# Attention and mixture of experts on one core: side work as emission threads, batch 1's loads moved, fill matmuls recounted

## The chip, the cores and the metric

The kernel runs on one core of one Trainium2 chip. The core has a matmul engine, TensorE (PE in the rows; PEld is its loading of stationary operands, which overlaps the matmuls), and three engines for element-wise work: VectorE (DVE), ScalarE (ACT) and GpSimd (POOL). SyncE (SP) issues the DMA transfers; its queue is SPq in the rows. Every engine executes its own list of instructions in order and waits on semaphores for the others. The metric is the device time of one execution in microseconds (us), lower is better.

## What is computed

Eight batches of 576 tokens go through an attention in two steps and then, token by token, through one of eight experts. Cut to what matters:

```python
def sm_attn(qq, kk, vv):
    s = scale * np.matmul(qq, kk.transpose(0, 1, 3, 2))
    a = np.exp(s - np.max(s, axis=-1, keepdims=True))
    a = a / (np.sum(a, axis=-1, keepdims=True) + 1e-09)
    return np.matmul(a, vv)
p_packed = sm_attn(p, k, v)              # p: 8 x 8 x 32 x 64;  q, k, v: 8 x 8 x 576 x 64
x = sm_attn(q, p_packed, p_packed)       # then 8 x 576 x 512
logits = np.einsum('bsd,de->bse', x, w_gate)                    # 8 experts
local_gate = 1.0 / (1.0 + np.exp(-np.einsum('bsd,de->bse', x, w_local).squeeze(-1)))
for b in range(B):
    prev_e = -1
    for s in range(S):
        fresh_e = int(np.argmax(logits[b, s]))
        e = fresh_e if s == 0 or local_gate[b, s] < 0.5 else prev_e
        prev_e = e
        h = np.maximum(x[b, s] @ w1[e], 0.0)                    # 512 -> 1024
        out[b, s] = softmax(logits[b, s])[e] * (h @ w2[e])      # 1024 -> 512
```

## The kernel before

**Work of one batch.** The 32 packed queries p attend to the keys (`scores`, the products at L374), the weights are raised to the exponent and transposed (`keys`, L419) and multiplied with the values (L428); a last transpose (L443) leaves `ppT`, the packed values turned, one tile for each of two groups of heads. The real queries are multiplied with `ppT` (`queries`, L469), and VectorE, ScalarE and GpSimd make the attention weights a2 of them: `a2t` in full, `a2h` its rounded high part (ScalarE, L509) and `a2l` the remainder (L512; on GpSimd, but for the second group of batch 0, which is on VectorE). GpSimd then copies 64 columns (L513), so that a2t is a whole number of 128-column blocks long, 640. The attention output itself is never formed: the gate weights are folded into `ppT` (`gate_weights`, L529, tile `gs`), and the gate products (`gates`, L600) are `a2t` times `gs`. The first token's expert is taken for the whole batch; a path behind a condition redoes tokens that need another one, and it isn't taken with these inputs. VectorE writes the expert's number (L543), SyncE reads it into a register (L546) and issues the two halves of w1 (`weights`, L689) and the eight blocks of w2 (L695). In the same way w1 is folded: `pack_weights` (L712) multiplies `ppT` with each half of w1, and ScalarE and VectorE split the result into a high part `wph` (L719) and a remainder `wpl` (L722).

**The main stream.** `chunks` goes over the 1,024 hidden units in eight chunks of 128. For each it makes two halves of 288 tokens of the hidden layer (`layer1`, L736, six matmuls a half: high by high, remainder by high, high by remainder, for two groups); ScalarE takes the relu (L741) and VectorE the remainder (L747, in `rest`). The matrix w2 is split likewise (`split`, L835 and L837). Then the products with w2 of the chunk before are added into five accumulators, acc0 to acc4 (`layer2`, L762, and L767 and L771 for the last 64 tokens). After chunk 7 `store` scales each accumulator by the gate's probability `pe` and writes it out.

**What sets the order.** Each engine's list is written when the program is built. `weave` holds a set of generators, each with a condition under which it may go on (`need`): `chunks` is the main one; others, for up to three batches at once, are loads, weights, packing, keys, scores, gates and queries. `Clock` estimates when each tile will be ready, from prices of instructions and rates of transfers, and `weave` lets the main one and the others take turns by these estimates and by a credit. Inside `chunks` the relu's remainder, the two parts of the split and the stores are written at fixed places between the blocks of `layer2` (`also`). SyncE's transfers stand in one list too: for batch 1 the first values come first, and `loads` holds back keys, packed queries and queries until all of batch 0's w2 is issued.

**The opening.** Before batch 0's first chunk there is nothing dense to multiply. `keep_warm` (L206) writes matmuls of zeros into a spare accumulator: five at the start, more when the estimated share of matmul time falls below a half, and, before each estimated wait, as many as the wait has stretches of 800 ns. Batch 0 differs in other ways (`early`): its keys are loaded in token order, its expert is found ahead of the queries by `early_choice` (L555 and L577) from the first token alone, and its queries are turned (L454) after that.

## Time and profile before

| | |
|---|---|
| median of 3 runs | 445.09 us (445.06 to 445.36) |
| the profiled execution | 444.92 us, of which the span of the profile is 443.1 |
| mean granted TensorE clock over the span | 0.970 |
| TensorE busy | 420.3 us, 95% |
| VectorE busy | 310.4 us, 70% |
| ScalarE busy | 177.0 us, 40% |
| GpSimd busy | 32.3 us, 7% |
| moved by DMA | 73.13 MB, 165 GB/s on average |

The profile is one execution. Its rows give instructions with start and length, or groups of them with the sum of busy time, the mean, and what ended the idle time ahead of them. The granted clock is TensorE's share of full speed (0.50 is 1.2 GHz, 1.00 is 2.4 GHz). A table by stage gives these for stretches of the span: batch 0's chunks run from 44.1 us to 84.3, batch 1's from 103.1 on, and from 202.5 to 427.7 the steady batches follow each other without a break.

### The profile page before, as it was taken

Reading aid. Unit: us, or ns where it says so; the run is one execution under the profiler, and the core shown is the slowest. Engines: PE = TensorE matmul, PEld = TensorE weight load, DVE = VectorE, ACT = ScalarE, POOL = GpSimd, SP = SyncE. Lnnn points to the kernel's source line nnn. Section 1 sums busy time; section 2 is a strip of 40 time slices with the busy share of each in tenths; the row PEclk is TensorE's granted clock in tenths of the full one; section 3 lists DMA queues with packets and bytes.
Section 4 is the critical chain, followed back from the end, with each engine's and each line's share of the span. In section 5 each row is a group of like instructions: output and inputs, shape, how many; then the busy total and the mean of one; then the engine's idle time right before and its main releaser. Section 6 shows DMA issues by size and latency. Waiting matters only on the chain.

```text
span 443.1 us, 9660 instructions
## 1 busy us (share of the span) xinstructions
PE 420.3 (95%) x3694; PEld 318.4 (72%) x3695; DVE 310.4 (70%) x834; ACT 177.0 (40%) x395; POOL 32.3 (7%) x55
## 2 busy tenths in 40 slices
...
GB/s 193 149 300 257 128 178 122 65 197 300 114 189 331 185 123 205 117 321 121 158 107 316 194 128 185 127 325 114 162 96 323 153 15 0 187 240 62 1 1 112
DMA packets 179380, 73.13 MB, mean 165 GB/s; under 512 B 151424, under 2 KB 158336, under 8 KB 179328
## 3 DMA queue, kind: packets, MB, share of 16 engines
...
q8 instruction: 31, 0.51, 0.6%
q10 hardware_dynamic: 2128, 0.15, 0.4%
q14 instruction: 21, 0.17, 0.2%
...
## 4 chain that ended last, share of the span: by engine, by line
PE 86%; DVE 6%; DMA 3%; ACT 1%; SPq 1%; issue 1%; POOL 0%; POOLq 0%; DVEq 0%
PE acc L762 41%; PE bank L736 23%; PE bank L712 3%; PE acc L767 3%; PE acc L771 3%; PE bank L428 3%; PE bank L469 2%; PE bank L419 2%; PE bank L374 2%; DMA kv<-in_k_dram 2%; PE bank L600 1%; DMA qn<-in_q_dram 1%; SPq L274 1%; PE acc L206 1%; DVE a L381 1%
## 5 line engine op out<-in xcount | busy, mean ns | idle before, releaser
L762 PE MATMUL acc<-w2s,h 128*128 128x512 f32 x768 | 208.0, 402 | 0.0
L762 PEld LDWEIGHTS acc<-w2s,h 128*128 128x128 f32 x768 | 134.9, 188 | 38.1 <-issue 13.8
L741 ACT ACTIVATE h<-bank 128x288 fp32r<-128x288 f32 x128 | 52.6, 411 | 166.7 <-PE bank L736 161.5
L747 DVE SCALAR_TENSOR_TENSOR h<-bank,h 128x288 fp32r<-128x288 f32 (+2 forms) x192 | 61.5, 348 | 54.4 <-ACT h L741 54.0
L736 PE MATMUL bank<-a2h,wph 128*128 128x288 f32 x256 | 78.7, 307 | 1.0 <-ACT a2h L509 0.4
L736 PE MATMUL bank<-a2h,wpl 128*128 128x288 f32 x256 | 76.4, 298 | 0.8 <-DVE wpl L722 0.8
L736 PE MATMUL bank<-a2l,wph 128*128 128x288 f32 x256 | 75.7, 296 | 1.1 <-POOL a2l L512 1.1
L736 PEld LDWEIGHTS bank<-a2h,wph 128*128 128x128 f32 x256 | 48.5, 189 | 19.7 <-issue 6.0
L736 PEld LDWEIGHTS bank<-a2l,wph 128*128 128x128 f32 x256 | 48.7, 190 | 5.7 <-POOL a2l L512 1.3
L736 PEld LDWEIGHTS bank<-a2h,wpl 128*128 128x128 f32 x256 | 48.6, 190 | 1.2 <-DVE wpl L722 1.2
L837 DVE TENSOR_TENSOR w2s<-w2raw,w2s 128x512 fp32r<-128x512 f32 x64 | 43.2, 675 | 5.6 <-ACT w2s L835 5.2
L512 POOL TENSOR_TENSOR a2l<-a2t,a2h 128x576 fp32r<-128x576 f32 x15 | 21.4, 1426 | 313.5 <-ACT a2h L509 278.6
L835 ACT CAST w2s<-w2raw 128x512 fp32r<-128x512 f32 x64 | 39.2, 613 | 0.2
L767 PE MATMUL acc<-w2s,h 128*128 128x512 f32 x64 | 25.8, 403 | 0.0
L771 PE MATMUL acc<-w2s,h 128*64 128x512 f32 x64 | 25.3, 396 | 0.0
L719 ACT CAST wph<-bank 128x512 fp32r<-128x512 f32 x30 | 16.1, 589 | 18.1 <-PE bank L712 18.1
L454 DVE STREAM_TRANSPOSE qn<-qn 128x1152 f32<-128x1152 f32 x16 | 21.8, 1367 | 0.5 <-DMA qn<-in_q_dram 0.5
L476 DVE STREAM_TRANSPOSE sT<-bank 128x288 f32<-128x288 f32 x31 | 13.2, 462 | 12.1 <-PE bank L469 11.9
L722 DVE TENSOR_TENSOR wpl<-bank,wph 128x512 fp32r<-128x512 f32 x30 | 19.2, 682 | 2.3 <-ACT wph L719 2.3
L500 DVE TENSOR_TENSOR sT<-sT,sm 128x576 f32<-128x576 f32 x16 | 18.9, 1187 | 0.3
L342 DVE STREAM_TRANSPOSE qn<-qn 128x1152 f32<-128x1152 f32 x14 | 19.0, 1357 | 0.1
L406 ACT ACTIVATE a<-a,nb 128x576 f32<-128x576 f32 x16 | 12.3, 772 | 11.4 <-DVE nb L392 11.4
(135 smaller groups left out, 411.8 us busy)
## 6 DMA issues: line engine op xcount, KB each, us to landing
...
kv<-in_v_dram SPq DMA_DIRECT2D x16, 576.0 KB, 10.5
...
```

The lines of the kernel that those rows point to most:

```text
L342: nc.vector.transpose(out=kT, in_=kT)
L454: nc.vector.transpose(out=qT, in_=qT)
L512: eng.tensor_tensor(out=a2l, in0=a2t[:, 0:S], in1=a2h.bitcast(F32), op=ALU.subtract)
L722: nc.vector.tensor_tensor(out=lo[:, Q], in0=ts[Q], in1=hi[:, Q].bitcast(F32), op=ALU.subtract)
L736: nc.tensor.matmul(out=t[:, :HALF], lhsT=st["wp"][c // 4][wi][:, Q, fs], rhs=a2[ai][Q][:, ts], start=(n == 0), stop=(n == 5),)
L741: nc.scalar.activation(out=h[:, ts], in_=t[:, :HALF], func=AF.Relu)
L747: nc.vector.scalar_tensor_tensor(out=h[:, dst:dst + z - a], in0=t[:, a:z], scalar=0.0, in1=h[:, HALF * half + a:HALF * half + z].bitcast(F32),
L762: nc.tensor.matmul(out=acc, lhsT=hs[hi], rhs=w[:, wi], start=(c == 0 and n == 0), stop=(c == NC - 1 and n == 2),)
L767: nc.tensor.matmul(out=acc, lhsT=h[:, 512:S + TAIL], rhs=w[:, 0], start=(c == 0), stop=False, skip_group_check=True,)
L771: nc.tensor.matmul(out=acc[0:TAIL], lhsT=h[:, 512:S], rhs=w[:, 1], start=False, stop=(c == NC - 1), skip_group_check=True,)
L835: nc.scalar.copy(out=w[:, 0], in_=raw)
L837: nc.vector.tensor_tensor(out=w[:, 1], in0=raw, in1=w[:, 0].bitcast(F32), op=ALU.subtract)
```

## The change

It has five parts.

1. **Threads.** What `chunks` wrote at fixed places is now a generator of its own, handed over with `aside`: `relu` (with the remainder), `split` and `store`. `weave` places them by the estimates, as it does the others. The blocks of `layer2` wait for the halves that they read.
2. **Loads.** Packed queries come before the keys in every batch but 0. For batch 1 keys are issued once two of batch 0's w2 blocks are, and queries once four are (`FIRST_W2`); the later w2 blocks wait for that.
3. **Gates.** From batch 1 on the gate weights are nine more columns in the bank of the queries' products, copied out by ScalarE into one of three kept tiles (`gate_all`). a2t is 576 columns long and GpSimd's copy is gone: the gate products are eight of 128 columns and eight of 32. Batch 1's no longer wait for batch 0's `pe` in the planner, and batch 0's chain behind its gates stands behind batch 1's choice.
4. **Opening.** A wait is filled with one matmul for each 450 ns. Both remainders of a2 go to VectorE in batch 0, and one of two copies behind the transposes too; 1/s is formed after the transposes instead of before; both groups' exponents are written before the first transposes.
5. **Turns.** Generators that want a PSUM bank may run twice as far ahead of ScalarE's and VectorE's estimated work; transfers are placed first; until batch 1's expert is chosen the credit doesn't hold the others back.

```diff
+FIRST_W2 = {"k": 2, "q": 4}
+GW = E + 1
...
+    gate_all = [const.tile([128, NQ, 32], F32, name=f"gate{x}") for x in range(3)]
...
-            order = (("v", 0), ("v", 1), ("k", 1), ("q", 1))
+            order = (("v", 0), ("v", 1), ("p", 1), ("k", 1), ("q", 1))
         for name, Q in order:
             blocks = name == "q" or (name == "k" and not st["early"])
-            if isinstance(b, int) and b == 1 and name == "k":
-                yield need(when=lambda: "w2" in sts[0])
-            yield need(slot="qn" if blocks else "kv")
+            if isinstance(b, int) and b == 1 and name in FIRST_W2:
+                yield need(when=lambda: len(sts[0].get("w2", ())) >= FIRST_W2[name])
...
         for r in range(2):
-            yield need(sc, banks=1)
+            yield need(sc, banks=1, when=lambda: not st["early"] or st["weighed"] == NQ)
...
-            nc.scalar.copy(out=a1T[:, J3 * r:J3 * r + J3],
-                           in_=tp[:TP, :128 * J3].rearrange("a (j x) -> a j x", j=J3))
+            copy = nc.vector.tensor_copy if st["early"] and r == 1 else nc.scalar.copy
+            copy(out=a1T[:, J3 * r:J3 * r + J3], in_=tp[:TP, :128 * J3].rearrange("a (j x) -> a j x", j=J3))
...
+        if not st["early"]:
+
+            for h in range(HQ):
+                nc.tensor.matmul(
+                    out=ts[0][32 * h:32 * h + 32, HALF:HALF + GW],
+                    lhsT=ppq[0:64, 32 * h:32 * h + 32],
+                    rhs=wgl[:, NQ * h + Q, 0:GW],
+                    start=True, stop=True,
+                )
+        if not st["early"]:
+            nc.scalar.copy(out=st["gate"][:, Q, 0:GW], in_=ts[0][:, HALF:HALF + GW])
...
-        eng = nc.vector if st["early"] and Q == 1 else nc.gpsimd
-        eng.tensor_tensor(out=a2l, in0=a2t[:, 0:S], in1=a2h.bitcast(F32), op=ALU.subtract)
-        nc.gpsimd.tensor_copy(out=a2t[:, S:SPAD], in_=a2t[:, SPAD - 128:S])
+        eng = nc.vector if st["early"] else nc.gpsimd
+        eng.tensor_tensor(out=a2l, in0=a2t, in1=a2h.bitcast(F32), op=ALU.subtract)
...
-        yield need(when=lambda: st["quads"] == NQ and "gs" in st and (expert is not None or st["b"] == 0 or "pe" in sts[st["b"] - 1]))
+        yield need(when=lambda: st["quads"] == NQ and "gs" in st and (expert is not None or st["b"] < 2 or "pe" in sts[st["b"] - 1]))
...
-                    out=lp[32 * i:32 * i + 32, :32 * NB],
-                    lhsT=gs[:, Q],
-                    rhs=a2t[Q].rearrange("a (n i t) -> a i n t", i=4, t=32)[:, i],
-                    start=(Q == 0), stop=(Q == NQ - 1),
+                    out=lp[32 * i:32 * i + 32, 0:128], lhsT=gs[:, Q],
+                    rhs=a2t[Q][:, 0:512].rearrange("a (n i t) -> a i n t", i=4, t=32)[:, i],
+                    start=(Q == 0), stop=False, skip_group_check=True,
+                )
+        for Q in range(NQ):
+            for i in range(4):
+
+                nc.tensor.matmul(
+                    out=lp[32 * i:32 * i + 32, 128:160], lhsT=gs[:, Q],
+                    rhs=a2t[Q][:, 512 + 32 * (i % 2):544 + 32 * (i % 2)],
+                    start=False, stop=(Q == NQ - 1), skip_group_check=True,
                 )
...
+        if st["early"]:
+
+            yield need(when=lambda: "ereg" in sts[1])
...
         for c in range(NC):
+            if st.get("early"):
+
+                yield need(when=lambda: all(c < n or x in sts[1] for x, n in FIRST_W2.items()))
             yield need(slot="w2raw")
...
-                hi, lo = st["wp"][c // 4]
-                yield need(hi, lo, *st["a2h"], *st["a2l"], banks=1)
-                h = tile_([128, 2 * S], F32R, "h")
-                rest = layer1(c, 0, h, st)
...
+                h, done = tile_([128, 2 * S], F32R, "h"), set()
+                for half, blocks in ((0, (0, 1, 2)), (1, (3, 4))):
+                    yield need(hi, lo, *st["a2h"], *st["a2l"], banks=1)
+                    aside(relu(layer1(c, half, st), half, h, done))
+                    if half == 0:
+                        st["begun"] = True
+                        raw, w = st["w2"][c], tile_([128, 2, DM], F32R, "w2s")
+                        aside(split(raw, w, done))
...
-            when = {x: t if x is main or x.loads else max(t, behind - (limit if x.batch <= soon else 0.0))
+            when = {x: t if x is main or x.loads else max(t, behind - limit * (2.0 if x.ready.banks else 1.0 if x.batch <= soon else 0.0))
                     for x, t in when.items()}
-            x = None
-            if credit >= 0.0 or when.get(main, 1e12) > now:
+            x = next((y for y, t in when.items() if y is not main and y.loads and t <= now), None)
+            if x is None and (credit >= 0.0 or "ereg" not in sts[1] or when.get(main, 1e12) > now):
...
-                    keep_warm(max(0, int((when[x] - now) / 800.0)))
+                    keep_warm(max(0, int((when[x] - now) / 450.0)))
```

**Three places in the order of instructions.** The number behind a name tells tiles of one name apart. First SyncE's list from batch 1's last early load to batch 2's values; `e0` is batch 0's expert. Before:

```order
L260 DMA kv_198<-in_v_dram 96x4x384
L546 TENSOR_LOAD e0_337
...
L689 DMA w1t_349<-in_moe_w1_dram 128x4x512
...
L695 DMA w2raw_353<-in_moe_w2_dram 128x512
...
L695 DMA w2raw_367<-in_moe_w2_dram 128x512
L274 DMA qn_370<-in_k_dram 32x72x32 x4
L291 DMA p_in_375<-in_p_dram 32x8x32 x4
L274 DMA qn_380<-in_q_dram 32x72x32 x4
L260 DMA kv_385<-in_v_dram 96x4x384
```

And with the change:

```order
L270 DMA kv_210<-in_v_dram 96x4x384
L301 DMA p_in_212<-in_p_dram 32x8x32 x4
L568 TENSOR_LOAD e0_357
...
L721 DMA w1t_370<-in_moe_w1_dram 128x4x512
...
L730 DMA w2raw_376<-in_moe_w2_dram 128x512
L284 DMA qn_378<-in_k_dram 32x72x32 x4
...
L730 DMA w2raw_385<-in_moe_w2_dram 128x512
L284 DMA qn_387<-in_q_dram 32x72x32 x4
...
L730 DMA w2raw_398<-in_moe_w2_dram 128x512
L270 DMA kv_400<-in_v_dram 96x4x384
```

Batch 1's four pack loads moved ahead of the read of the expert's register, its keys ahead of six of the eight w2 blocks and its queries ahead of four.

Second TensorE's list where batch 0's chunks end (acc4 of chunk 6's products) and batch 1's begin; `a2t_548` and `a2t_568` are batch 1's, `qn_420` and `qn_444` batch 2's keys. Before:

```order
L771 MATMUL acc4_600<-w2s_953,h_944 64x512
L600 MATMUL bank1_1043<-a2t_548,gs_906 32x160 x4
L600 MATMUL bank1_1043<-a2t_549,gs_906 32x160 x4
L374 MATMUL bank0_1063<-qn_420,p_in_425 32x288 x4
...
L419 MATMUL bank2_1153<-ident_72,a1_1061 96x128 x3
...
L428 MATMUL bank0_1188<-kv_385,a1T_1100 32x64 x24
...
L469 MATMUL bank1_1230<-qn_711,ppT_1224 32x288 x4
...
L712 MATMUL bank0_1262<-w1t_1117,ppT_802 32x512 x4
...
L712 MATMUL bank0_1326<-w1t_1119,ppT_802 32x512 x4
...
L736 MATMUL bank2_1339<-a2h_550,wph_1260 128x288
```

And with the change, first the gates (among the products of the chunk before, chunk 5), then the end of the chunks:

```order
L809 MATMUL acc3_601<-w2s_908,h_898 128x512 x3
L622 MATMUL bank1_987<-a2t_568,gate1_90 32x128 x4
...
L630 MATMUL bank1_987<-a2t_569,gate1_90 32x32 x4
L814 MATMUL acc4_610<-w2s_908,h_898 128x512
...
L818 MATMUL acc4_610<-w2s_954,h_946 64x512
L385 MATMUL bank1_1139<-qn_444,p_in_404 32x288 x4
...
L427 MATMUL bank0_1208<-ident_72,a1_1137 96x128 x3
L747 MATMUL bank2_1215<-w1t_1056,ppT_728 32x512 x4
...
L427 MATMUL bank0_1227<-ident_72,a1_1137 96x128 x3
L439 MATMUL bank0_1252<-kv_400,a1T_1207 32x64 x24
L770 MATMUL bank2_1279<-a2h_570,wph_1213 128x288
```

Batch 1's gate products moved from behind the last block of batch 0's chunk 6 to between two blocks of chunk 5. Batch 2's queries, second transposes and second values, and the second packing, left the stretch ahead of batch 1's first L770.

Third TensorE's list in the opening, from the early choice to the second packing of batch 0. Before:

```order
L529 MATMUL acc3_303<-wgl_85,ppT_293 32x32 x4
L206 MATMUL acc4_66<-warm_64 128x256 x2
L577 MATMUL acc0_121<-gs_312,et_324 32x32 x2
L206 MATMUL acc4_66<-warm_64 128x256 x3
L469 MATMUL bank0_394<-qn_110,ppT_289 32x288 x4
...
L206 MATMUL acc4_66<-warm_64 128x256 x2
L712 MATMUL acc2_440<-w1t_349,ppT_289 32x512 x4
L712 MATMUL acc3_441<-w1t_349,ppT_293 32x512 x4
L206 MATMUL acc4_66<-warm_64 128x256 x4
L712 MATMUL bank0_480<-w1t_351,ppT_289 32x512 x4
```

And with the change:

```order
L551 MATMUL acc3_322<-wgl_85,ppT_312 32x32 x4
L210 MATMUL acc4_66<-warm_64 128x256 x4
L599 MATMUL acc0_127<-gate0_89,et_342 32x32 x2
L210 MATMUL acc4_66<-warm_64 128x256 x7
L480 MATMUL bank0_418<-qn_116,ppT_308 32x288 x4
...
L210 MATMUL acc4_66<-warm_64 128x256 x5
L747 MATMUL acc2_462<-w1t_370,ppT_308 32x512 x4
L747 MATMUL acc3_463<-w1t_370,ppT_312 32x512 x4
L210 MATMUL acc4_66<-warm_64 128x256 x6
L747 MATMUL bank0_503<-w1t_372,ppT_308 32x512 x4
```

Nothing moved here; the fill matmuls between the same neighbours became more, 2, 3, 2 and 4 before and 4, 7, 5 and 6 now.

## Rows read from the trace of the kernel before

**Rows 1.** The page, part 1: busy us of each engine (share of the span) and instructions.

```profile
PE 420.3 (95%) x3694; PEld 318.4 (72%) x3695; DVE 310.4 (70%) x834; ACT 177.0 (40%) x395; POOL 32.3 (7%) x55
```

**Rows 2.** Table by stage: us, busy (instructions) of PE, PEld, DVE, ACT, POOL; PEclk, DMA, GB/s.

```profile
44.10:84.30 40.20, 40.20 (x370) 31.57 (x366) 31.16 (x86) 14.39 (x35) 2.14 (x2) 1.00 1.10 136
...
84.30:103.10 18.80, 13.96 (x224) 6.44 (x223) 15.41 (x52) 6.73 (x17) 1.96 (x4) 0.73 0.51 186
...
202.50:427.70 225.20, 224.90 (x1904) 175.26 (x1903) 156.62 (x416) 93.98 (x210) 16.56 (x24) 1.00 0.65 147
```

**Rows 3.** Timeline of TensorE, passage: start, us, instruction, passes, [idle before, releaser].

```profile
87.44 0.47 PE L600 MATMUL bank<-a2t,gs 128*32 128x160 f32 x4 [1.90 <-POOL a2t L513]
```

**Rows 4.** The chain of waits at full clock: start, us, piece.

```profile
124.32 0.68 PE bank L600 x16
...
131.41 0.65 PE bank L374 x16
...
140.12 0.66 PE bank L419 x6
...
141.24 1.02 PE bank L712 x16
...
148.05 0.81 PE bank L428 x48
...
158.51 0.26 PE bank L529 x16
...
404.54 2.09 PE acc L762 x9
...
409.37 2.09 PE acc L762 x9
```

**Rows 5.** VectorE and SyncE queue: batch 1's expert, issue of w1, landing; batch 2's issue.

```profile
91.52 0.14 DVE L543 TENSOR_SCALAR e<-codes_all 1x1 int32<-1x1 f32 x1
...
92.45 1.01 SPq L689 DMA_DIRECT2D w1t<-in_moe_w_dram  x2
...
DMA to landing us min/median/max: 5.1/6.1/7.2
...
133.44 1.08 SPq L689 DMA_DIRECT2D w1t<-in_moe_w_dram  x2
```

**Rows 6.** Table by stage, stretches of 2 us, columns as in rows 2.

```profile
30.00:32.00 2.00, 0.16 (x8) 0.16 (x16) 1.92 (x4) 1.25 (x2) 0.00 (x0) 1.00 1.05 387
...
42.00:44.00 2.00, 2.00 (x21) 1.23 (x19) 0.52 (x2) 0.92 (x2) 0.00 (x0) 0.50 1.32 128
...
88.00:90.00 2.00, 2.00 (x32) 0.45 (x23) 1.86 (x9) 0.22 (x1) 0.00 (x0) 0.61 0.00 0
```

**Rows 7.** Timeline of TensorE and VectorE in the opening.

```profile
1.23 6.31 PE L206 MATMUL acc<-warm 128*128 128x256 f32 x16 [1.23 <-DVE warm L199]
...
8.96 1.15 PE L374 MATMUL acc<-kv,p_in 32*32 32x192 f32 x48 [1.42 <-DVE p_in L333]
...
22.85 2.93 PE L206 MATMUL acc<-warm 128*128 128x256 f32 x6
...
32.87 2.00 PE L206 MATMUL acc<-warm 128*128 128x256 f32 x8
...
24.38 2.64 DVE L454 STREAM_TRANSPOSE qn<-qn 128x1152 f32<-128x1152 f32 x2 [0.47 <-DMA qn<-in_q_dram]
```

**Rows 8.** Timeline of SyncE queue, VectorE and TensorE: batch 1's keys, end of chunk 0.

```profile
35.19 9.29 SPq L274 DMA_DIRECT2D qn<-in_k_dram  x4
...
49.35 1.38 DVE L342 STREAM_TRANSPOSE qn<-qn 128x1152 f32<-128x1152 f32 x1
...
48.04 0.40 PE L771 MATMUL acc<-w2s,h 128*64 128x512 f32 x1
```

**Rows 9.** VectorE: one a2l subtraction; L500, same kind and shape, ns min/median/max.

```profile
36.94 1.35 DVE L512 TENSOR_TENSOR a2l<-a2t,a2h 128x576 fp32r<-128x576 f32 x1 [0.74 <-ACT a2h L509]
...
L500 DVE TENSOR_TENSOR sT<-sT,sm x16: 744/757/1981, 33.3 to 371.7; 128x576 f32<-128x576 f32 x16
```

135 lines of the change are left out of this document (70 added, 65 removed), and 2 rows, old and new, of the table BUFS.

## The prediction

> **What bounds the kernel now.** I read the page first: TensorE is busy for 420.3 of 443.1 us [rows 1], so the question is only where the rest lies and what of the 420 is slow. The table by stage answers it [rows 2]: from 202.5 to 427.7 us the matmul engine is busy 224.9 of 225.2 us at a granted clock of 1.00, and from 44.1 to 84.3 it has no gap at all. Between these stands the passage from batch 0 to batch 1, 84.3 to 103.1: 18.8 us, of which the engine is busy 14.0, at a clock of 0.73. The timeline shows how it begins [rows 3]: after batch 0's last block the engine stands in batch 1's gate products (L600) until 87.4, the last 1.9 us for GpSimd's copy of 64 columns (L513). Batch 1's first product (L736) comes only at 103.1, the end of the stage. The chain of waits gives what the same pieces cost elsewhere at full clock [rows 4]: gates 0.68, scores 0.65 a half, transposes 0.66, weighted values (L428) 0.81, gate weights 0.26, one queries group as long as one of scores, packing 1.02 a half. In the passage stand gates, 2 scores, 2 transposes, 2 L428, gate weights, 1 queries, 2 packings: 0.68 + 1.30 + 1.32 + 1.62 + 0.26 + 0.65 + 2.04 = 7.9 us. So **10.9 us are lost in the passage** (18.8 - 7.9). Its cause is a chain: batch 1's chosen expert is known at 91.66, the SyncE queue issues the first half of w1 at 92.45, and it lands 5.1 us later [rows 5]. Nothing useful is left to multiply, the clock falls (0.61 over 88 to 90, [rows 6]) and stays low.
>
> The other loss is the opening, until 44.1, which runs at half clock in places ([rows 6]: 0.50 from 42 to 44). The steady batches and the end offer nothing but fewer matmul instructions.
>
> **The change part by part.** The sum is made against the profiled execution (444.92 us, span 443.1); the median of the three runs is 0.17 above it.
>
> *A, opening and batch 0.* Three things happen. (1) The fill matmuls at the head grow from 8 to 14. Eight take 6.31 us from 1.23; at the later rate of 0.50 each (8 passes in 2.00) six more end at 7.54 + 3.0 = 10.5, while the first scores started at 8.96 [rows 7]: 1.6 us late. In return the clock may hold through the transposes and L428, which took 4.6 us instead of 1.32 + 1.62 = 2.9: 1.7 back. What follows is not limited by this chain anyway: VectorE's query transposes start at 24.38 after a 0.47 us wait for the query load [rows 7]. (2) Batch 1's four pack loads now stand on SyncE before the read of batch 0's expert, and batch 1's keys after w2 chunk 1 instead of chunk 7. In the trace the keys are issued from 35.19 for 9.29 us and VectorE turns them at 49.35 [rows 8]. Six w2 chunks are 1.5 MB, 4 us at the 387 GB/s of the row of 30 to 32 [rows 6]; less 0.5 to 1 for the packs, the keys land some 3 us sooner and are turned by about 47.7. The new order asks for the first scores of batch 1 right after chunk 0's last block, which ended at 48.3 [rows 8]. So it fits, but the keys now set the pace: a faster opening would gain at most 0.5, a slower one costs in full. (3) The rest of a2 (L512) for both halves goes to VectorE. The trace has one such on VectorE, 1.35 us, while instructions of this kind and shape take 0.75 at their shortest [rows 9]; two would be 1.5 to 2.7 in place of 1.35 plus GpSimd's wait. I take 1.5, since GpSimd's like instruction no longer runs beside it. The Trainium skill (SBUF — State Buffer, Who interferes with whom) says that a VectorE instruction with two SBUF inputs and a GpSimd one that reads SBUF exclude each other. By that the 1.35 was half waiting and the sum keeps 1.5; without it A would be 1.2 us worse. *A = 0, from a gain of 0.5 to a loss of 3.*
>
> *B, the passage.* With scores at chunk 1 instead of 2, queries at chunk 3 instead of 4 and 5, and GpSimd's column copy gone, batch 1's gates stand one chunk and 0.46 us ahead of the passage (the order shows them between two blocks of chunk 5). A chunk is 4.83 us 409.37 - 404.54, [rows 4], so T, the passage's start, is 5.3 us after the gates. From the gates' end (87.9) the trace takes 4.5 us to the issue of w1 and 5.1 to its landing [rows 3, 5], so w1 lands at T + 4.3. Packing ends at T + 5.4; cast, subtraction and the L428 that stands ahead take it to T + 7.3 for batch 1's first product (two casts and a subtraction lag a packing by about 1.5). Work inside: 2 scores, 1 transposes, 1 packing, 1 L428 = 1.30 + 0.66 + 1.02 + 0.81 = 3.8. Loss left: 3.5. During the 3 us wait before the packing the engine idles as it did from 85.5 to 87.4, after which the clock fell; I therefore charge a half-clock stretch like the one of 40.6 to 44.0 on dense work: 3.4 us at half rate, 1.7 us. *B = 10.9 - 3.5 - 1.7 = a gain of 5.7*; 7.4 if the clock holds; 3 if the dense rows run slow for 8 us.
>
> *C, all batches.* Seven batches lose the separate gate-weight products (0.26 each, 1.8 in all) and get the same number of narrower ones beside the queries; the gates of eight batches become 8 + 8 products instead of 8, at most another 0.26 each, 2.1. From -1.8 to +2.1 I take 0: the narrow ones follow products of their own kind. Relus, remainders, splits and stores as threads of their own issue the same instructions; the matmul engine hides them (no wait of it is listed after 103), and the last rows of the matmul order are the same as before. But packing moves up: in the new order it stands behind the gates by 9.7, 10.9, 9.2, 11.1, 10.9 and 8.5 us of matmul work in batches 2 to 7, where gates to landing takes 9.6. The short ones can wait 0.4 and 1.1. *C = a loss of 0.5, from a gain of 1.8 to a loss of 3.6.*
>
> **Sum:** 0 + 5.7 - 0.5 = 5.2 us; 444.92 - 5.2 = 439.7, and on the median 439.9.
>
> **The rivals.**
> *Everything falls into place.* The clock holds in the passage (7.4), the keys come in time (0.5), C is neutral: 7.0 to 9.5 us, 435.4 to 437.9. For it: from 30 to 32 the engine was busy 0.16 us and the clock stayed at 1.00 [rows 6]. Against: after the gap before 87.4 it fell.
> *The fill is the bound.* From 20.2 to 26.7 the fill ran at half rate, 0.49 a pass (6 passes in 2.93) [rows 7], although it left hardly a gap. Behind the early choice the fill grows from 3 to 7 matmuls, 14 passes: 3.5 us at full rate, 6.9 at half. At half the queries' products start 3 us after 25.86 and the whole chain to batch 0 follows, with 1 to 3 us kept after the keys' slack: 441.7 to 443.8. The Trainium skill (TensorE: Matmul & The Clock Gate, Part 1: The HAM clock gate) says that sustained activity releases the throttle, which would put the fill at full rate and A at 0; the trace shows a stretch of fill that did not bring it up at once.
> *The loads come no sooner.* The DMA engines' share is 1.10 over 44 to 84 us [rows 2], so moving keys ahead only moves others back; if batch 2's queries still land at 84 and w1 queues behind them, w1 lands where it would at 89 to 90 and half of B stays: 443.0 to 445.3.
> *Slower: packing waits for w1 in every batch.* SyncE issues in order, and the stores of the batch before and the next loads stand ahead of w1. For batch 2 the trace has w1 issued at 133.44, 8.4 us after the gates' end at 125.0 [rows 4, 5], not 4.5. If earlier gates meet the same queue, landing is 13.5 after the gates; half of that delay (11.6) makes waits of 1.9 + 0.7 + 2.4 + 0.5 + 0.7 + 3.1 = 9.3, so 449; all of it 460. It decides from 1.5 us of delay in each batch. Against: the planner moves stores and loads with the rest, and in the steady batches before the queue was free.
>
> **How the numbers follow.** Forecast (437.9 to 441.7) 0.47; everything in place 0.20; fill as bound 0.15; loads no sooner 0.06; slower 0.12. The range goes from 435.8 to 443.9 and leaves out the very best end, most of the third rival and the slower one. About 0.2% (0.9 us) is what a measurement of this kernel can tell from no change; faster than that 0.84, within 0.04, slower 0.12.
>
> **What would show it.** Right: batch 1's first L770 product near 92 to 94 with 3 us of pending batch 2 work behind it; gates (L622) of batch 1 near 78; w1 issued 4 to 5 us later; a wait of L747 or of the transposes of 2 to 4 us near 84 to 88 and a granted clock of 0.5 just after. In the opening: L480 starting at 26 to 27, the first L809 at 42 to 45. Wrong: waits of L747 on w1 in later batches; scores of batch 1 waiting on the keys past 49; fill at 0.49 a pass between 20 and 30; any matmul idle after 110 beyond 1.5 us.

## The result and the profile after

Timed in turns, twenty executions each, the changed kernel took 443.9 us (median; 438.87 to 446.23) and the kernel before 445.9 (444.31 to 447.35). The ratio of undisturbed executions is 0.9939, with a 95% interval from 0.9921 to 0.9958. On the scale of the prediction, where the kernel before stood at 445.09, that is 442.4 us: a gain of 2.7 us (1.9 to 3.5), where 5.2 were forecast. The direction was right, the size about twice too large.

The changed kernel spreads over 7 us, the one before over 3, and the time goes with the mean granted clock: the five executions below 441.5 us had a mean clock of 0.981 to 0.988, those above 444 had 0.970 to 0.974. The first profiled execution was the slowest of the twenty (446.23 us), so the readings rest on a second one (441.45 us, the run "a1_again" below), and the first is shown where the two differ. Side by side:

| us | before | after, first | after, second |
|---|---|---|---|
| span | 443.1 | 444.5 | 439.7 |
| batch 0's first layer-2 product (L762; now L809) starts at | 44.12 | 45.36 | 44.16 |
| from there to the start of the last L771 (now L818) | 387.34 | 387.63 | 383.88 |
| of it TensorE idle | 5.2 | 6.3 | 6.4 |
| of it lost to half clock | 4.3 | 6.0 | 1.5 |
| of it the rest | 377.8 | 375.4 | 376.0 |

Idle is the stretch less TensorE's busy time; half-clock loss is half the busy time of the stretches at a granted clock of 0.50; the rest is what remains. The last line is matmul work at full clock, and it fell by about 2 us. Idle time did not fall. Between the two executions half clock is 4.5 of the 4.8 us of span.

The page's first part (as [rows 1]), first execution, then the table by stage of the second one, columns as in [rows 2]: batch 0's chunks, the passage up to batch 1's first L770, and all behind it.

```profile
PE 424.1 (95%) x3860; PEld 329.2 (74%) x3861; DVE 309.1 (70%) x837; ACT 176.4 (40%) x400; POOL 24.5 (6%) x41
```

```profile
44.16:87.42 43.26, 41.26 (x400) 32.85 (x399) 32.25 (x82) 15.67 (x38) 3.23 (x4) 1.00 1.21 153
87.42:97.14 9.72, 6.59 (x103) 2.56 (x103) 7.88 (x45) 3.92 (x11) 0.37 (x2) 0.82 1.03 366
97.14:428.04 330.90, 329.68 (x2910) 259.95 (x2907) 237.75 (x630) 142.81 (x324) 19.82 (x24) 1.00 0.73 160
```

Against [rows 2], batch 0's chunks are 3.1 us longer and have 2.0 us of gaps where they had none; the passage is 9.7 us instead of 18.8, of which 3.1 idle.

**The opening**, TensorE and VectorE of the second execution, as [rows 7]:

```profile
15.03 1.32 PE L439 MATMUL bank<-kv,a1T 96*32 96x64 f32 x78
18.66 0.49 PE L439 MATMUL bank<-kv,a1T 96*32 96x64 f32 x18 [2.31 <-issue]
20.78 3.29 PE L210 MATMUL acc<-warm 128*128 128x256 f32 x8
24.00 0.31 PE L599 MATMUL acc<-gate,et 128*32 128x32 f32 x4
```

```profile
22.69 0.24 DVE L596 STREAM_TRANSPOSE et<-es 128x64 f32<-128x64 f32 x1
25.16 0.14 DVE L565 TENSOR_SCALAR e<-ecd 1x1 int32<-1x1 f32 x1
```

The clock did hold through the transposes, and the products of the weighted values (L439) start sooner (15.03 against 15.50), but in the midst of them TensorE stands still for 2.31 us for nothing that the profile shows, and they end at 19.15 where they ended at 18.68. Then four fill matmuls run partly at half clock, and the early choice's product, whose input is ready at 22.93, comes at 24.00. In the first execution these four took 3.78 us and the expert was known at 26.09 (here and below the start of the instruction that writes it, L565). VectorE's query transposes follow right behind, at 25.33 and 26.26, where they started at 24.38 before.

**Batch 1's keys**, SyncE's queue, VectorE and TensorE of the second execution, as [rows 8]:

```profile
26.30 1.05 SPq L721 DMA_DIRECT2D w1t<-in_moe_w_dram  x2
...
29.91 12.25 SPq L284 DMA_DIRECT2D qn<-in_k_dram  x4
```

```profile
47.61 1.38 DVE L353 STREAM_TRANSPOSE qn<-qn 128x1152 f32<-128x1152 f32 x1 [2.35 <-DMA qn<-in_k_dram]
48.91 0.40 DVE L344 STREAM_TRANSPOSE p_in<-p_in 128x256 f32<-128x256 f32 x1
49.23 1.34 DVE L353 STREAM_TRANSPOSE qn<-qn 128x1152 f32<-128x1152 f32 x1
50.49 0.48 DVE L785 SCALAR_TENSOR_TENSOR h<-bank,h 128x224 fp32r<-128x224 f32 x2
```

```profile
49.37 0.81 PE L385 MATMUL bank<-qn,p_in 64*32 64x288 f32 x16 [1.00 <-DVE p_in L344]
51.12 0.37 PE L770 MATMUL bank<-a2h,wph 128*128 128x288 f32 x1 [0.95 <-DVE h L785]
```

The keys are issued 5.3 us sooner than before (29.91 against 35.19), the issue takes 12.25 us instead of 9.29, and they are turned 1.7 us sooner (0.5 in the first execution). VectorE waits 2.35 us for them, then turns them (1.38, 0.40 and 1.34 us) with the relu's remainder (L785) behind, and TensorE has two gaps: 1.00 us for the scores' operands, 0.95 for the remainder.

**The passage**, VectorE and SyncE from the gates' transpose to the issue of batch 1's w1, then TensorE:

```profile
81.99 0.34 DVE L637 STREAM_TRANSPOSE lt<-bank 128x160 f32<-128x160 f32 x1
82.25 1.34 DVE L353 STREAM_TRANSPOSE qn<-qn 128x1152 f32<-128x1152 f32 x1
83.51 0.65 DVE L798 TENSOR_TENSOR w2s<-w2raw,w2s 128x512 fp32r<-128x512 f32 x1
84.08 0.45 DVE L785 SCALAR_TENSOR_TENSOR h<-bank,h 128x288 fp32r<-128x288 f32 x1
84.45 0.18 DVE L645 TENSOR_REDUCE gmx<-lt 128x5 f32<-128x40 f32 x1
...
85.37 0.14 DVE L565 TENSOR_SCALAR e<-codes_all 1x1 int32<-1x1 f32 x1
```

```profile
86.30 1.01 SPq L721 DMA_DIRECT2D w1t<-in_moe_w_dram  x2
```

```profile
89.14 0.69 PE L385 MATMUL bank<-qn,p_in 64*32 64x288 f32 x8 [0.79 <-DVE h L785]
90.06 0.69 PE L385 MATMUL bank<-qn,p_in 64*32 64x288 f32 x8 [0.23 <-DVE a L392]
91.98 0.88 PE L427 MATMUL bank<-ident,a 128*96 128x128 f32 x3 [1.23 <-ACT a L417]
92.79 1.96 PE L747 MATMUL bank<-w1t,ppT 64*32 64x512 f32 x16
...
96.29 0.88 PE L439 MATMUL bank<-kv,a1T 96*32 96x64 f32 x48 [0.88 <-ACT a1T L429]
```

The gate products moved ahead as planned. Their chain on VectorE has a hole of 2.1 us (from the transpose's end at 82.33 to the first reduction, L645, at 84.45), in which batch 2's keys, a split and a remainder run. From the gates' end to w1's issue it still takes the 4.4 us of the forecast (4.5 before); an unbroken chain would save the hole, it is no loss against the forecast. The gaps in the passage are waits for VectorE and ScalarE on batch 2's scores; none is for w1. How the clock then behaves decides the execution. Two-microsecond stretches, the second execution, then the first (whose passage begins 2.7 us later):

```profile
92.00:94.00 2.00, 2.00 (x19) 0.65 (x19) 1.85 (x20) 0.47 (x1) 0.00 (x0) 0.50 1.06 387
96.00:98.00 2.00, 1.71 (x55) 1.62 (x55) 1.46 (x4) 1.50 (x4) 0.00 (x0) 1.00 1.05 386
```

```profile
94.00:96.00 2.00, 1.31 (x11) 0.68 (x19) 1.85 (x17) 1.02 (x3) 0.00 (x0) 0.50 1.05 393
100.00:102.00 2.00, 2.00 (x26) 1.83 (x19) 0.95 (x2) 0.22 (x1) 0.00 (x0) 0.50 1.08 378
```

The same gaps cost 3.4 us at half clock in the one and 10.2 in the other.

### The profile page after: what moved, and what is told of

Read it like the earlier page. It is cut to its first block, busy times and chain, and to the rows that moved or that the text cites. A ratio compares the mean times of both kernels' runs of the same rounds, so it can differ in the third digit from the quotient of the medians.

```text
span 444.5 us, 9978 instructions
## 1 busy us (share of the span) xinstructions
PE 424.1 (95%) x3860; PEld 329.2 (74%) x3861; DVE 309.1 (70%) x837; ACT 176.4 (40%) x400; POOL 24.5 (6%) x41
## 4 chain that ended last, share of the span: by engine, by line
PE 81%; DVE 6%; DMA 4%; SPq 3%; issue 2%; ACT 1%; POOLq 0%; POOL 0%; DVEq 0%
PE acc L809 38%; PE bank L770 22%; PE bank L747 3%; PE bank L439 3%; PE acc L814 3%; PE acc L818 3%; SPq L284 2%; PE bank L427 2%; DVE qn L353 2%; PE bank L480 2%; PE bank L385 2%; DMA p_in<-in_p_dram 2%; DMA qn<-in_k_dram 2%; DMA kv<-in_k_dram 1%; DVE h L785 1%
## 5 line engine op out<-in xcount | busy, mean ns | idle before, releaser
L809 PE MATMUL acc<-w2s,h 128*128 128x512 f32 x768 | 209.1, 403 | 0.0
L809 PEld LDWEIGHTS acc<-w2s,h 128*128 128x128 f32 x768 | 136.2, 190 | 31.6 <-issue 8.6
L785 DVE SCALAR_TENSOR_TENSOR h<-bank,h 128x288 fp32r<-128x288 f32 (+2 forms) x192 | 61.3, 346 | 43.4 <-ACT h L780 42.5
L770 PE MATMUL bank<-a2h,wph 128*128 128x288 f32 x256 | 78.3, 306 | 2.6 <-DVE df L680 1.2
L770 PE MATMUL bank<-a2h,wpl 128*128 128x288 f32 x256 | 76.1, 297 | 0.0
L770 PE MATMUL bank<-a2l,wph 128*128 128x288 f32 x256 | 75.6, 295 | 0.0
L770 PEld LDWEIGHTS bank<-a2h,wph 128*128 128x128 f32 x256 | 48.4, 189 | 18.7 <-issue 7.3
L770 PEld LDWEIGHTS bank<-a2l,wph 128*128 128x128 f32 x256 | 48.6, 190 | 4.5
L798 DVE TENSOR_TENSOR w2s<-w2raw,w2s 128x512 fp32r<-128x512 f32 x64 | 47.1, 736 | 3.1 <-ACT w2s L796 2.8
L770 PEld LDWEIGHTS bank<-a2h,wpl 128*128 128x128 f32 x256 | 48.5, 189 | 0.0
L535 POOL TENSOR_TENSOR a2l<-a2t,a2h 128x576 fp32r<-128x576 f32 x14 | 20.5, 1465 | 329.9 <-ACT a2h L532 329.9
L818 PE MATMUL acc<-w2s,h 128*64 128x512 f32 x64 | 25.3, 395 | 0.0
L210 PE MATMUL acc<-warm 128*128 128x256 f32 x78 | 23.9, 469 | 1.2 <-DVE warm L203 1.2
L210 PEld LDWEIGHTS acc<-warm 128*128 128x128 f32 x78 | 18.1, 240 | 5.7 <-issue 1.6
L353 DVE STREAM_TRANSPOSE qn<-qn 128x1152 f32<-128x1152 f32 x14 | 19.0, 1358 | 2.4 <-DMA qn<-in_k_dram 2.4
L447 DVE TENSOR_SCALAR zz<-bank,rs 128x128 f32<-128x128 f32 x16 | 5.6, 351 | 19.9 <-PE bank L439 19.8
```

The lines of the kernel that those rows point to most:

```text
L210: nc.tensor.matmul(out=warm_ps[:, :256], lhsT=warm[:, :128], rhs=warm, start=True, stop=True)
L353: nc.vector.transpose(out=kT, in_=kT)
L535: eng.tensor_tensor(out=a2l, in0=a2t, in1=a2h.bitcast(F32), op=ALU.subtract)
L770: nc.tensor.matmul(out=t[:, :HALF], lhsT=st["wp"][c // 4][wi][:, Q, fs], rhs=a2[ai][Q][:, ts], start=(n == 0), stop=(n == 5),)
L785: nc.vector.scalar_tensor_tensor(out=h[:, dst:dst + z - a], in0=t[:, a:z], scalar=0.0, in1=h[:, HALF * half + a:HALF * half + z].bitcast(F32),
L798: nc.vector.tensor_tensor(out=w[:, 1], in0=raw, in1=w[:, 0].bitcast(F32), op=ALU.subtract)
```

## The experiments

The theory after the result, as it stood before these runs: the loads' order gained little, since the keys' landing is set by what the DMA engines move, and VectorE's queue gives back what the earlier gates gained; what is left of the passage is gaps and, above all, the clock that falls in them. Rivals: the fill matmuls are what costs; the moved loads are what gains; the landing of w1 ends the passage in any case. Each kernel is the changed one with one edit, but a1_again is the changed one itself, a13_both has two edits, and b1_loads is the kernel before with one part of the change. Most of the runs have intervals that overlap the changed kernel's; where they do, a difference of the medians is not shown to be one of the kernels. Ratios are to the kernel before on the same chip. The last two columns are idle time and half-clock loss from the first layer-2 product on, worked out as above, in the profiled execution.

| run | median us | ratio (95%) | first L809 | idle | half clock |
|---|---|---|---|---|---|
| a1_again | 443.01 | 0.9955 (0.9935 to 0.9974) | 44.16 | 6.4 | 1.5 |
| a2_fill800 | 444.64 | 0.9966 (0.9944 to 0.9988) | 42.48 | 7.7 | 6.2 |
| a4_loads8 | 444.60 | 0.9980 (0.9968 to 0.9992) | 45.38 | 5.4 | 5.8 |
| a5_turn_late | 443.56 | 0.9953 (0.9932 to 0.9973) | 44.24 | 6.2 | 4.6 |
| a6_nofill_choice | 442.89 | 0.9930 (0.9906 to 0.9954) | 46.08 | 4.5 | 3.1 |
| a7_gates_first | 443.88 | 0.9965 (0.9940 to 0.9990) | 42.28 | 8.9 | 2.6 |
| a8_keys_first | 446.06 | 1.0032 (1.0002 to 1.0061) | 49.95 | 2.9 | 2.3 |
| b1_loads | 448.75 | 1.0060 (1.0036 to 1.0084) | 44.72 | 7.5 | 6.2 |
| a9_gates0_now | 441.44 | 0.9912 (0.9878 to 0.9946) | 44.09 | 3.8 | 3.4 |
| a11_nofold | 447.68 | 1.0040 (1.0013 to 1.0066) | 44.75 | 4.8 | 4.2 |
| a12_fill_passage | 440.30 | 0.9885 (0.9845 to 0.9925) | 44.32 | 5.2 | 0.0 |
| a13_both | 440.83 | 0.9888 (0.9864 to 0.9913) | 45.39 | 3.7 | 0.0 |
| a14_pack_ahead | 442.83 | 0.9929 (0.9906 to 0.9953) | 45.34 | 4.9 | 3.9 |

**The changed kernel again.**

> The changed kernel once more, unchanged. Theory: its executions differ only in where the granted clock falls to half; what is not the clock stays. So the median is 441.5 to 444.5 us, the second values products (L439) again stop until 18.4 to 18.7 us, the first L809 starts at 44.5 to 46, batch 1's keys are turned (L353) from 48.5 to 49.2, and TensorE again waits 1.5 to 2.5 us between 49 and 53. Rival: the stops between 49 and 53 are themselves an accident of the profiled execution; then there is no wait there, batch 0's last L818 comes near 86 instead of 89.7, and the time is below 441.

The median and the gaps (1.00 and 0.95 us) came as expected; the first L809 and the keys came some 0.5 to 1 us sooner than the ranges. The gaps of batch 0 are no accident.

**Less fill.**

```diff
-                    keep_warm(max(0, int((when[x] - now) / 450.0)))
+                    keep_warm(max(0, int((when[x] - now) / 800.0)))
```

> One edit of the changed kernel: a wait in the opening is filled with one matmul for each 800 ns again instead of 450 (8, 1, 2, 3, 2, 4 fill matmuls as in the kernel before, instead of 14, 3, 4, 7, 5, 6). Theory fill in the way: the four fill matmuls ahead of the early choice's product L599 at half clock (3.78 us) hold the expert back by 1.6 us and the chain behind it; with two it is known at 23.6 to 24.6 us instead of 26.1, the first L809 starts 1 to 2 us sooner (43.3 to 44.4) and the time falls by 1 to 2 us. Rival clock: the fill buys clock; with less of it the granted clock is at half for longer, L599 and the first L809 come no sooner (45 or later) and the time rises by 0 to 3 us. The stop of the second values products ends at 18.4 to 18.7 in either case, if it is the fetch of instructions, but stands 16 matmul records later in the row (94 and 2 instead of 78 and 18).

```profile
18.29 0.27 PE L439 MATMUL bank<-kv,a1T 96*32 96x64 f32 x2 [2.21 <-issue]
...
48.96 0.81 PE L385 MATMUL bank<-qn,p_in 64*32 64x288 f32 x16 [2.27 <-DVE p_in L344]
```

In this execution the chain did as the theory said: the expert at 23.66, the first L809 1.7 us sooner. That the smaller fill did it isn't shown: a7_gates_first below, whose opening is the changed kernel's, has the expert at 23.29 and the first L809 at 42.28, and the runs with an unchanged opening range from there to 45.39. The time didn't follow (444.64): TensorE stands 2.27 us for the keys instead of 1.00, in a7_gates_first 1.91. An opening that comes out early is mostly given back at the keys. And the stop of the values' products ends at about the same time (18.29, 18.66 in a1_again), sixteen matmul records later in the list.

**No fill ahead of the choice.**

```diff
-                    keep_warm(max(0, int((when[x] - now) / 450.0)))
+                    keep_warm(max(0, int((when[x] - now) / (1e6 if "gs" in sts[0] and "ereg" not in sts[0] else 450.0))))
```

> One edit of the changed kernel: no fill matmuls between the gate weights and the early choice's product L599, and one fewer behind it; all other fill as changed. Theory keys: the expert is known 1.5 to 2 us sooner (23.8 to 24.6 us) and the first L809 starts 1 to 2 us sooner (42 to 43.5), but batch 1's keys still land at 48.5 to 49, so TensorE's gap for them grows by as much (2 to 2.5 us ahead of the first scores), batch 0's last L818 ahead of the passage stays at 86.5 to 88.5, and the time is within 1 us of the changed kernel's. Rival fill: the fill ahead of the choice is what costs, and without it the time falls by 1.5 to 2 us.

The expert came at 24.77, only 0.4 us ahead of the second execution, and the first L809 at 46.08, behind a half-clock stretch from 42.2 on; the step expected there failed, though one execution can't tell it from the spread of the opening. The time is the changed kernel's. Keys were turned at 47.72, and TensorE hardly waited for them (0.3 us), as it came late itself.

**Loads back behind w2.**

```diff
-FIRST_W2 = {"k": 2, "q": 4}
+FIRST_W2 = {"k": 8, "q": 8}
```

> One edit of the changed kernel: batch 1's keys and queries are issued after all eight w2 blocks of batch 0 again. In the order of instructions batch 1's scores then stand at chunk 2, its gates in chunk 6's products instead of chunk 5's, and the passage has four score groups and both packings in a row. Theory keys: the gap and the half clock of 50 to 57 us vanish, so batch 0's second L818 follows the first L809 by 8.5 to 9.5 us (16.4 now), which gives 3 to 4 us; the later gates take 3 to 5 us in the passage (14 to 15 us from batch 0's last L818 to batch 1's first L770, 10.8 now). Sum within 1.5 us of the changed kernel. Rival loads: the moved loads carry the gain of the change, and without them the time goes back to that of the kernel before, 2 to 3 us up.

Batch 0's second L818 follows the first L809 by 8.8 us, with no gap; in the passage the first L770 follows the last L818 of chunk 6 by 11.3 us instead of 10.1. The median is 1.6 us above the changed kernel's beside it, the ratio 0.25% higher, with intervals that just overlap: the moved loads are worth about 1 us, less than half of the gain, and not clearly more than nothing. Here the gates come a chunk later, yet the choice is known about as far ahead of the passage's start (1.1 us ahead of the last L818, 1.6 in a1_again), since VectorE goes through the chain without a break:

```profile
83.82 0.35 DVE L637 STREAM_TRANSPOSE lt<-bank 128x160 f32<-128x160 f32 x1 [0.66 <-PE bank L630]
...
85.14 0.14 DVE L565 TENSOR_SCALAR e<-codes_all 1x1 int32<-1x1 f32 x1
```

**Loads early, key transposes late.**

```diff
-            yield need(when=lambda: "k" in st and "p" in st and (not isinstance(st["b"], int) or sts[0]["quads"] == NQ))
+            yield need(when=lambda: "k" in st and "p" in st and (not isinstance(st["b"], int) or (sts[0]["quads"] == NQ and sts[0].get("c", 0) >= 2)))
```

(`c` is the chunk of batch 0.)

> One edit of the changed kernel: the loads stay where they are, but VectorE's transposes of batch 1's keys may not be placed ahead of chunk 2 of batch 0. Theory placing: keys land at 48.5 to 49 as now, VectorE no longer waits for them with the relu's remainders behind it, TensorE has no gap between 48 and 56, and batch 0's second L818 follows the first L809 by 8.5 to 9.5 us; scores at chunk 2 and gates one chunk later, passage 14 to 15 us as with the loads moved back, and the time is within 1 us of that run's. Rival loads: loads issued early are worth something by themselves (w2 blocks and queries land in another order), and this run is 2 us or more below the one with the loads moved back.

No gap from the first L810, which is L809 here, to the second tail product (9.5 us); one of 0.57 us comes at 61.55. The median is 1.0 us below the run with the loads moved back and 0.5 above the changed kernel, both within the intervals. Early scores bought nothing that can be seen over late ones without a gap.

**Keys ahead of w1.**

```diff
+            order = (("p", 1), ("k", 1), ("v", 0), ("v", 1), ("q", 1)) if isinstance(b, int) and b == 1 else (("v", 0), ("v", 1), ("p", 1), ("k", 1), ("q", 1))
...
+FIRST_W2 = {"k": 0, "v": 2, "q": 4}
```

> One edit of the changed kernel: batch 1's packed queries and keys are issued right behind batch 0's queries, ahead of the read of the expert and of w1, and its values after two w2 blocks instead. Theory DMA: the order of transfers only shifts what waits. Keys land near 30 us instead of 48.7 and no wait for them is left, but SyncE is held by their issue until 28 to 30, w1 is issued 2 to 4 us later (29 to 31.5 instead of 26.3 to 27.2), the first L809 starts at 46 to 48, and the time is within 1.5 us of the changed kernel. Rival slack: batch 0's packing has 4 us of slack behind VectorE's chain, so the first L809 moves by less than 1 us and the time falls by 2 to 4 us.

```profile
37.51 1.96 PE L747 MATMUL acc<-w1t,ppT 64*32 64x512 f32 x16 [5.19 <-DMA w1t<-in_moe_w_dram]
```

No wait for keys is left and idle time is the lowest of all (2.9 us), but w1 is issued at 30.75 and the first L809 starts at 49.95, later than either theory said: 3 us slower than the changed kernel. What is moved for batch 1 first, batch 0 waits for here.

**The loads alone, in the kernel before.**

```diff
-            order = (("v", 0), ("v", 1), ("k", 1), ("q", 1))
+            order = (("v", 0), ("v", 1), ("p", 1), ("k", 1), ("q", 1))
...
+            if isinstance(b, int) and b == 1 and name in FIRST_W2:
+                yield need(when=lambda: len(sts[0].get("w2", ())) >= FIRST_W2[name])
```

> The kernel before with one part of the change alone: batch 1's packed queries ahead of its keys, keys after two and queries after four of batch 0's w2 blocks, instead of all after the eight. Theory: the loads are about half of the gain; batch 1's scores stand at chunk 1, its gates (L601 here) come earlier than the passage, the passage shrinks from 18.8 us to 12 to 16, batch 0's chunks get 1 to 4 us longer, and the time is 0.5 to 2 us below the kernel before. Rival threads: the gain comes from the relus, splits and gates in other places; the loads alone give nothing (within 0.5 us) or cost up to 2 us, since VectorE waits for the keys here as well.

```profile
88.02 1.42 PE L375 MATMUL bank<-qn,p_in 64*32 64x288 f32 x16 [2.36 <-DVE p_in L334]
89.37 1.28 PE L601 MATMUL bank<-a2t,gs 128*32 128x160 f32 x12
```

Slower by 0.6%. The old planner puts batch 2's scores (L375) ahead of batch 1's gates (L601), which come at 89.4 instead of 84.4. In the old planner the loads alone cost time; that the turns which the rest of the change gives to gates are what makes them pay fits this, but is argued from this one run.

**Batch 2's keys behind the packing.**

```diff
-(not isinstance(st["b"], int) or sts[0]["quads"] == NQ))
+(not isinstance(st["b"], int) or (sts[0]["quads"] == NQ and (st["b"] != 2 or len(sts[1].get("wp", ())) > 0))))
```

> One edit of the changed kernel: VectorE's transposes of batch 2's keys, and with them batch 2's scores, may not be placed ahead of batch 1's first packing. Theory VectorE queue: batch 1's gate chain then runs on VectorE without the 1.3 us of key transposes ahead of it, the expert is known 2.5 to 3.2 us behind the transpose of the gate products (L637; 3.4 to 3.8 now), w1 is issued 1 to 1.5 us sooner against the passage's start, packing starts when it lands, 3 to 4.5 us behind batch 0's last L818 ahead of the passage instead of 5.6 to 5.8, and batch 1's first L770 follows that L818 by 7 to 8.5 us instead of 8.5 to 10.8. Time 1 to 3 us below the changed kernel, if batch 2's scores fit later. Rival w1: the landing of w1 ends the passage whatever stands on VectorE; TensorE then stands idle for 4 us or more, the clock falls, and the time is the same or up to 2 us longer.

```profile
90.04 1.96 PE L747 MATMUL bank<-w1t,ppT 64*32 64x512 f32 x16 [3.68 <-DVE pe L704]
92.67 0.61 PE L770 MATMUL bank<-a2h,wph 128*128 128x288 f32 x1 [0.67 <-ACT wph L754]
```

The choice comes 2.7 us behind the gates' transpose (3.4 in a1_again), the packing starts when w1 has come, 5.4 us behind its issue at 84.62 (the profile names `pe`, whose instruction ended beside it, at 90.03, but the packing doesn't read `pe`; w1's first half landed 5.3 us behind its issue), and batch 1 starts 6.7 us behind the mark instead of 10.1. And the time isn't better: the wait for w1 is now bare, and batch 2's scores are work that still has to be done. The rival was right here: a shorter passage is no gain where it only puts the covering work behind it.

**Batch 0's gate chain at once.**

```diff
-        if st["early"]:
-
-            yield need(when=lambda: "ereg" in sts[1])
```

> One part of the change undone: batch 0's gate chain on VectorE no longer waits in the order for batch 1's choice, and so stands around batch 1's key transposes again. Theory VectorE queue: in the passage VectorE has some 3 us less to do between batch 1's choice and batch 2's scores, the two waits of TensorE on it there (0.8 and 0.2 us) and the one on the exponent behind them (1.2) shrink to under 1.2 us together, batch 1's first L770 follows batch 0's last L818 ahead of the passage by 7 to 9 us (8.5 to 10.8 now), and the time falls by 1 to 3 us. Batch 0's chain fits in VectorE's idle time ahead of the keys, so batch 0's chunks don't get longer. Rival w1: its landing ends the passage, and the order of VectorE changes nothing there; the time stays within 1 us, or rises by up to 2, since batch 1's scores now stand behind the gate chain.

The median is 1.6 us below the changed kernel's on another chip, with overlapping intervals, and it comes by another way than expected in part: w1 is issued as late as before against the passage, and the two waits on scores stay (0.8 and 1.0 us). What went is the wait on the exponent, as the packing now stands ahead of batch 2's transposes, and all of batch 0's gaps: the keys are turned between pieces of the gate chain (L353 from 46.64), the scores come later in chunk 1, and TensorE doesn't wait.

**Gate weights apart again.**

```diff
-        if not st["early"]:
-            for h in range(HQ):
-                nc.tensor.matmul(
-                    out=ts[0][32 * h:32 * h + 32, HALF:HALF + GW],
...
-                    gate_weights(st) if started == 0 else None, gates(st)
+                    gate_weights(st), gates(st)
```

> One part of the change undone: the gate weights are products and a bank of their own again in every batch, not columns beside the queries. The rest of the order is the same. Theory fold: the matmul time without idle time and half clock, from the first L809 to the last L818, was 377.8 us before the change and 375.3 to 376.6 with it; the fold takes 1.8 of it (seven times 0.26), so this run has 377 to 378.2, and the time is 1 to 2.5 us above the changed kernel's. Rival tiles: the narrow products cost as much as the wide ones, and the 2 us come from elsewhere (fewer changes between kinds of products, the split gates); then this run has 375.3 to 376.6 as well.

The rest came to 382.2 us, 6 more than with the fold, far outside both ranges. The order did not stay the same: in a steady batch the transposes L427, six in a row in the changed kernel, come in groups of three. Two lines of a steady batch:

```profile
236.19 1.31 PE L385 MATMUL bank<-qn,p_in 64*32 64x288 f32 x16
...
255.94 0.33 PE L539 MATMUL bank<-wgl,ppT 64*32 64x32 f32 x16
```

The separate products themselves are 0.33 a batch, 2.3 in seven; one of the batch's two score groups takes 1.31 us here, the other 0.71 (0.72 in the changed kernel). How much of the 2 us that the change saved is the fold itself stays open.

**Zeros in the passage**, and a kernel with the packing ahead but no zeros.

```diff
+        if isinstance(st["b"], int) and st["b"] == 2:
+            for _ in range(2 + Q):
+                nc.tensor.matmul(out=ts[1][:, HALF:512], lhsT=warm[:, :128], rhs=warm[:, :512 - HALF], start=True, stop=True)
```

> One addition to the changed kernel: two and three matmuls of zeros behind batch 2's two score groups, in columns of their bank that are not used, so that TensorE multiplies where it waits in the passage. (The first packing then stands ahead of batch 2's first transposes in the order.) Theory clock: idle time in the passage falls from 3 us to under 2, the granted clock is at half for at most one stretch of 3.4 us there in most executions, so the slow end of the spread (445 to 446) goes and the median falls by 1 to 2.5 us. Rival: the fill and the early wait for w1 hold back the work behind them by as much, and the half clock still comes, as the fill of the opening didn't prevent it from 19 to 25 us; time within 1 us or up to 2 above.

```diff
-            yield need(sc, banks=1, when=lambda: not st["early"] or st["weighed"] == NQ)
+            yield need(sc, banks=1, when=lambda: (not st["early"] or st["weighed"] == NQ) and (not isinstance(st["b"], int) or st["b"] != 2 or len(sts[1].get("wp", ())) > 0))
```

> One edit of the changed kernel, no matmuls of zeros: batch 2's transposes may not be placed ahead of batch 1's first packing, which thus stands right behind batch 2's scores, as in the two faster runs. Theory clock: the matmuls of zeros were what gained; with the order alone TensorE stands still for 2 to 3 us ahead of the packing, the clock falls there for two or three stretches, and the time is within 1 us of the changed kernel (442.5 to 444.5). Rival order: that the packing no longer stands behind the transposes, and so behind batch 2's exponent, is what gained; the time falls to 440 to 442.

In both, as in a9_gates0_now, the packing is ahead of batch 2's transposes. TensorE of a12_fill_passage (its lines behind the three added ones are numbered 3 higher; each of its five added matmuls has two records) and one stretch of it, then one stretch of a14_pack_ahead and one of a9_gates0_now:

```profile
88.50 1.02 PE L393 MATMUL bank<-warm 128*128 128x224 f32 x4
89.46 1.51 PE L385 MATMUL bank<-qn,p_in 64*32 64x288 f32 x16
90.90 1.40 PE L393 MATMUL bank<-warm 128*128 128x224 f32 x6
92.23 1.09 PE L750 MATMUL bank<-w1t,ppT 64*32 64x512 f32 x16
```

```profile
94.00:96.00 2.00, 0.91 (x5) 0.68 (x5) 1.91 (x14) 1.95 (x5) 0.00 (x0) 1.00 1.05 383
```

```profile
94.00:96.00 2.00, 0.88 (x3) 0.46 (x3) 1.96 (x9) 1.03 (x3) 0.00 (x0) 0.50 1.05 386
92.00:94.00 2.00, 2.00 (x14) 0.51 (x3) 1.37 (x7) 1.04 (x2) 0.00 (x0) 0.50 1.05 387
```

The first two stretches have about the same busy share; the clock is 1.00 in the one and 0.50 in the other. With the zeros there is no half-clock stretch from 44 us to the end, and the time falls to 440.3; a14_pack_ahead has 442.83, which is the changed kernel's. But the two differ in more than the zeros: behind the first packing a12_fill_passage goes straight to batch 1's products (L773 at 94.00), a14_pack_ahead to batch 2's transposes (L427 at 92.79) and only at 97.97 to batch 1's (L770). The order of a12_fill_passage without zeros is that of a9_gates0_now (packing at 90.63, batch 1's first product at 93.41), so the pair that differs in the zeros alone is a9_gates0_now and a13_both:

> Two edits together: batch 0's gate chain not held back for batch 1's choice, and the five matmuls of zeros in the passage. Theory, that waits and clock are separate losses: each edit alone left the other's (3.8 us of idle time behind the first L809 and two half-clock stretches with the one, 5.2 us and none with the other); together 3 to 4.5 us of idle time and at most one such stretch, span 437 to 439, median 438.5 to 440.5. Rival: the matmuls of zeros take the place of the idle time that the other edit removes and hold back the packing; median 440 to 442.

Against a9_gates0_now the half-clock loss falls from 3.4 us to none and the idle time stays (3.8 and 3.7). It is so beyond the profiled executions: the mean granted clock is 0.981 to 0.989 in all twelve executions with the zeros, 0.973 to 0.987 in the fourteen of a9_gates0_now and a14_pack_ahead. The gain in time is small: from the first layer-2 product to the end of the span 383.8 us became 382.0, the median 441.44 became 440.83, with overlapping intervals. The zeros themselves hold TensorE for 2.4 us (1.02 + 1.40 in the lines above). So zeros kept the clock up, and what that is worth in time is between nothing and some 2 us.

Against the zeros alone, the median with both edits is no better. The span of the profiled execution was as expected (438.9), the median 0.3 above the range. The gains don't add: in its profile the first L809 starts at 45.39, behind a half-clock stretch from 41.8 on that the profile of a12_fill_passage lacks; whether that is so in all its executions wasn't seen. a12_fill_passage and a13_both have the lowest medians of this study, with a9_gates0_now 0.6 to 1.1 us behind.

## Why the prediction was half right

The direction and the two places of gain and loss, the passage and the opening, were right; three steps of the sum failed. In A the keys were to be turned 3 us sooner, and came 0.5 and 1.7 us sooner with their cost to TensorE put at nothing. In B the wait that is left was put on w1, and it is on batch 2's scores, with a half clock that was charged once and came one to three times. In C the matmul work was to stay, and it fell by about 2 us.

*The loss in the passage* was put at 10.9 us. Idle time and half clock there come to 4.8 + 4.3 = 9.1; the other 1.8 is the passage's pieces taking 9.7 us at full clock where their price among others is 7.9. The chain was read rightly: gates' end to w1's issue took 4.4 us in the first execution (4.5 forecast).

*Term B, forecast 5.7.* Idle and half clock in the passage are 3.0 + 4.3 us in the first execution and 3.1 + 1.5 in the second, so B was 1.8 and 4.5, not counting some 0.5 us by which the passage's pieces came closer to their price. The mechanism held (gates two blocks into chunk 5, w1 early), but two steps failed. The wait of 3 us was put on w1; it is on batch 2's scores (0.79 and 0.23 us, then 1.23 and 0.88 for ScalarE's work on them), whose VectorE work (the transposes of its keys and packed queries, L353 and L344, and a relu's remainder) stands ahead of them, and batch 1's first product came 10.3 and 9.7 us behind the passage's start instead of 7.3. Batch 0's delayed gate chain is not shown as the cause of that: without it, in a9_gates0_now, the two waits stay (0.8 and 1.0 us). And the half clock was charged with one stretch of 3.4 us, where executions have one to three; a13_both against a9_gates0_now takes 3.4 us of loss away and gives 0.6 us of the median.

*Term A, forecast 0 with a loss of up to 3.* It was a loss of 5.0 in the first execution (1.2 in the first L809, 2.1 in gaps, 1.7 at half clock in batch 0's chunks) and of 2.0 in the second, all in gaps. The step that failed is the keys: "3 us sooner" were 0.5 and 1.7. What was issued sooner took longer to issue (12.25 us, not 9.29; a4_loads8, whose keys go out at 36.86, has 9.20). That the DMA engines were full, which they look to be at a share of 1.00 and more, is the likely cause, and no run shows it alone. The second gap was put at nothing: VectorE's work on the keys stands ahead of the relu's remainder, and TensorE waits 0.95 us for that. "The keys now set the pace" was right: in a2_fill800 a first L809 1.7 us sooner brings the first scores only 0.4 us sooner (48.96 against 49.37). That what follows is "not limited by this chain anyway" was wrong: VectorE's query transposes start right behind the choice, 1.0 and 1.9 us later than before, and the queries' products (L480) at 27.5 and 28.6 instead of 26 to 27. a2's remainders were sized well: two on VectorE took 1.48 us together in the first execution (1.5 forecast), half of it each, where one beside GpSimd's took 1.35 [rows 9]. This agrees with the Trainium skill (SBUF — State Buffer, Who interferes with whom), by which a VectorE instruction with two inputs in SBUF and a GpSimd one that reads SBUF hinder each other.

*Term C, forecast a loss of 0.5.* It was a gain: matmul work at full clock fell from 377.8 to 375.4 and 376.0. Some 0.5 us of that lie in the passage, and 0.8 us of new short waits behind the passage go off, so about 0.5 to 1 us are left. The wait that was feared did not come. TensorE's waits behind 42 us in the second execution, whole list:

```profile
PE bank L427 <- ACT a L417: 1.2, 1, 1.2
PE bank L770 <- DVE df L680: 1.2, 2, 0.6
PE bank L385 <- DVE p_in L344: 1.0, 1, 1.0
PE bank L770 <- DVE h L785: 0.9, 1, 0.9
PE bank L439 <- ACT a1T L429: 0.9, 1, 0.9
PE bank L385 <- DVE h L785: 0.8, 1, 0.8
PE bank L385 <- DVE a L392: 0.2, 1, 0.2
```

There is no L747 on w1 among them, so the slower rival never arose.

*The rivals.* "The loads come no sooner" (0.06) was nearly right on the keys and wrong on w1. "The fill is the bound" (0.15) gave the range in which the time lies, 441.7 to 443.8, but not its cause: the fill that was in the way stood ahead of the early choice, and in a2_fill800 and a6_nofill_choice its removal gains nothing; that the time lies in its range is luck. Of the prediction's signs of being wrong two came true: the fill ran partly at half rate between 20 and 25, and batch 1's scores waited on the keys past 49. In all, A's loss and a smaller B, with a better C, left half.
